# Attention and SwiGLU layer on one core: staging in two tags, final sums spread, two queues left to the scheduler

## The chip, the cores and the metric

The kernel runs on one core of a Trainium2 chip. The metric is the device time of one execution in microseconds (us), given as the median of the runs shown.

A core has five engines that work side by side, each through its own queue of instructions in order: TensorE (PE, matmuls; its weight loads are listed as PEld), VectorE (DVE), ScalarE (ACT), GpSimd (POOL) and SyncE (SP), which issues nearly all transfers here. An instruction starts when it is at the head of its queue and the semaphores that it waits for have come.

## The reference, cut to what matters

One sequence of 2048 rows with 576 columns goes through attention with 32 query heads and 16 key heads over the last 512 keys of a cache, then through a SwiGLU MLP with 4608 hidden columns. Both are gated by vectors computed from a condition c. All data are fp32.

```
mod = (silu(c) @ w_mod).reshape(1, 6, 1, -1)          # sa, ca, ga, sb, cb, gb
h = layernorm(x) * (1 + ca) + sa
q = (h @ wq) in 32 heads of 128                       # wq: 576 x 4096
k, v = k_cache[:, :, -512:], v_cache[:, :, -512:]     # 16 heads, each used twice
o = softmax(q k^T * 128**-0.5) v                      # 2048 x 4096
x = x + ga * (o @ wo)                                 # wo: 4096 x 576
h = layernorm(x) * (1 + cb) + sb
out = x + gb * ((silu(h @ w1) * (h @ w3)) @ w2)       # w1, w3: 576 x 4608, w2: 4608 x 576
```

## The kernel before

**Split numbers.** A matmul operand is kept as a rounded high part and the low rest. `split` (L82) makes them: ACT casts the high part (L84), another engine subtracts it from the source (L85). A product is then three matmuls, or seven for the 576-deep ones.

**Attention** runs in 128 slots, one for each head and block of 512 rows: first blocks 0 and 1, then blocks 2 and 3, with the two blocks of a head in successive slots. A slot has four steps t. In each, PE makes the scores of 128 rows (`scores`, L315 to L317), turns an earlier slot's exponentials (`turn`, L335), projects the next slot's q (`query`, L266) and multiplies an earlier slot's result with wo (`attend_out`, `back`, L282). ACT casts the turned exponentials to their high part (pth, L336), DVE subtracts the low part (ptl, L342), and DVE adds the result into acc (L366). Per head wq is loaded three slots and split two slots ahead of its first use (wh on ACT, wl on POOL with L85); wo is loaded (L229), weighted by gate_a (POOL, L773) and split into o. Per two heads K and V are loaded the same way. gate_a and gate_b are made on PE (`mod_rows`, L146); gate_b belongs to slot 9.

**Preparation.** The MLP needs its weights as operand sets of a seven-product scheme with sums and differences of quarter blocks, high and low parts each. These sets are made during attention and written to DRAM. For each of 36 chunks f of 128 hidden columns `load_raw` (L471, L474) loads the raw blocks, POOL makes sums (L483 to L487), and `make_set` makes seven sets, each with an ACT cast (L489) into a staging tile wmade, two POOL subtractions (L490, L491) and a write on SP (L492, to wd). For each pair of chunks `load_rows` (L519) loads rows of w2, POOL weights them by gate_b and makes sums (L538 to L543), and `keep` stages seven tiles omade: ACT cast L525, POOL L526, write L529 to od. Staging tiles are buffers of tag xn, ST = 4 of them. A cast can start only when the write of the tile four before it has landed.

The 385 items are put into the steps of slots 8 to 56, 66 to 74 (`early`, five items to four steps) and 85 to 116 (`late`). Raw loads are issued six steps ahead of the first set, row loads eleven steps ahead of the first tile. Their tag hs has seven buffers, which also hold w_mod blocks and normalized rows.

**MLP.** It runs in two pairs of row blocks, 36 groups each, one group per chunk (pair 0: groups 0 to 35, pair 1: 36 to 71). d counts the pairs of chunks, j is the chunk in it. A group has seven products (`product`, L570: sums py and px), and after each a few of the 14 units of `down` (L648: pe and pf) for the chunk pair before, whose results DVE adds into sums (L636). `act_steps` splits the activations for these units (aah, aal, akv), mostly on POOL. Weight sets come on SP by L563, w2 rows by L558.

At the end of a pair the sums are combined: `finish` has five POOL additions per 128-row tile (L592 to L596), `finish_first` one (L603), and for pair 0 the results are stored (L607). `down` calls these directly behind units 6 to 13 of d = 17 and d = 34. The last chunk pair has its own path, `plain` (L658).

**What sets the order.** ORDERED (L34) lists the engines whose instructions are issued in the order in which the program writes them. An engine that is not in the list is ordered by the scheduler, which runs the program through a model of its own and gives a free engine the earliest written operation that is ready there. Buffers of a tag are handed out in written order. `at(i, t, task)` puts a task behind step t of slot i, or behind product t of group ("m", g); t = -1 is ahead of the first.

Of the kernel before, what the change touches and what calls it, by code (L numbers as in the profile page):

```python
# [9 lines left out]
F32R = mybir.dt.float32r  # L10
# [6 lines left out]
P = 128  # L17
D = 576
DC = 4
# [4 lines left out]
ST = SB // P  # L24
# [5 lines left out]
HALF = D // 2  # L30
EPS = 1e-5
PB, QB, RB, HB = 4, 1, 3, 7

ORDERED = {mybir.EngineType.PE, mybir.EngineType.DVE, mybir.EngineType.Activation, mybir.EngineType.Pool, mybir.EngineType.SP}  # L34
SCALE = float(DH) ** -0.5


# [1 line left out]
def tile_block(  # L39
# [14 lines left out]
    nc = tc.nc  # L54
# [405 lines left out]

    wdram = {(f, k): dram.tile([P, DC + 1, P], F32, name=f"wd{f}{k}") for f in range(NF) for k in ORDER}
    works = {}

    def load_raw(f):

# [11 lines left out]
    def make_set(f, n):  # L477


        a11, a12, a21, a22, s1, s2 = (works[f][:, k] for k in range(6))  # L480
        k, x = (("p1", a11), ("p2", a12), ("p4", a22), ("p5", s1), ("p6", s2), ("p7", a21), ("p3", a12))[n]
        if n == 0:
            nc.gpsimd.tensor_add(s1, a21, a22)  # L483
            nc.gpsimd.tensor_sub(s2, s1, a11)
        elif n == 2:
            nc.gpsimd.tensor_sub(a21, a11, a21)
            nc.gpsimd.tensor_sub(a12, a12, s2)  # L487
        t = pool.tile([P, DC + 1, P], F32R, tag="xn", name="wmade", bufs=ST)
        nc.scalar.copy(t[:, :3, :], x)  # L489
        nc.gpsimd.tensor_sub(t[:, 3:, :], x[:, :2, :], t[:, :2, :].bitcast(F32))  # L490
        nc.gpsimd.tensor_sub(t[DR:, 2, :], x[DR:, 2, :], t[DR:, 2, :].bitcast(F32))  # L491
        nc.sync.dma_start(wdram[f, k][:, :, :], t.bitcast(F32))  # L492
        if n == 6:
            del works[f]
# [6 lines left out]
    G = NF // 2  # L501
# [19 lines left out]

    def keep(x, to, also=None):

        t = pool.tile([P, 2, HALF], F32R, tag="xn", name="omade", bufs=ST)
        nc.scalar.copy(t[:, 0, :], x)  # L525
        nc.gpsimd.tensor_sub(t[:, 1, :], x, t[:, 0, :].bitcast(F32))  # L526
        for dst in (to, also):
            if dst is not None:
                nc.sync.dma_start(dst, t.bitcast(F32))  # L529
# [47 lines left out]
    def split_act(d, k, x, eng):  # L577
        tags = ("ah", "al") if k in ("p7", "p4", "p6") else ("kv", "kv")
        hi, lo = [pool.tile([P, SB], F32R, tag=t, name=f"a{t}", bufs=8 if t == "kv" else 3) for t in tags]
        split(hi, lo, x, eng)  # L580
        halves[d, k] = hi, lo
# [6 lines left out]
    def finish(pair, t, eng):  # L588

        m15, m6 = msums[pair][0][t], msums[pair][1][t // 2][:, t % 2, :]  # L590
        a = half_split(acc[2 * pair + 1][:, t, :])
        eng.tensor_add(m6, m6, m15[:, 0, :])  # L592
        eng.tensor_add(a[:, 1, :], a[:, 1, :], m6)
        eng.tensor_add(a[:, 0, :], a[:, 0, :], a[:, 1, :])
        eng.tensor_add(a[:, 1, :], a[:, 1, :], m15[:, 1, :])
        eng.tensor_add(m15[:, 1, :], m15[:, 1, :], m6)  # L596
        if pair == 0:
            store_out(1, t)

    def finish_first(pair, t, eng):  # L600

        a = half_split(acc[2 * pair][:, t, :])
        eng.tensor_add(a, a, msums[pair][0][t])  # L603

    def store_out(b, t):
        lo = b * SB + t * P
        nc.sync.dma_start(out[0, lo : lo + P, :], acc[b][:, t, :])  # L607
# [3 lines left out]
    def down(d, u):  # L611

        pair = d // G
        lane[0] += 1
        ps = lane[1][lane[0] % 2]
        if u < 4:
            q, t = 0, u
            jobs = [("p4", 0, t), ("p7", 1, t)]
            into = half_split(acc[2 * pair + 1][:, t, :])
        elif u < 6:  # L620
            q, t = 1, u - 4
            jobs = [("p6", 0, 2 * t), ("p6", 0, 2 * t + 1)]
            into = msums[pair][1][t]
        elif u < 10:
            q, t = 2, u - 6
            jobs = [("p1", 0, t), ("p5", 1, t)]
            into = msums[pair][0][t]
        else:
            q, t = 3, u - 10
            jobs = [("p2", 0, t), ("p3", 1, t)]  # L630
            into = half_split(acc[2 * pair][:, t, :])
        multiply(ps, [(halves[d, k], osets[d, q][:, i], r) for k, i, r in jobs])
        if d % G == 0 and q in (1, 2):
            nc.vector.tensor_copy(into, ps[:, :, :HALF])
        else:
            nc.vector.tensor_add(into, ps[:, :, :HALF], into)  # L636
        if d == G - 1 or d == 2 * G - 2:
            if q == 2:
                finish(pair, t, nc.gpsimd)
            elif q == 3 and pair == 0:  # L640
                finish_first(0, t, nc.vector)
                store_out(0, t)

    def multiply(ps, jobs):
        for h, ((lh, ll), w, r) in enumerate(jobs):
# [18 lines left out]
    def act_steps(g, k):  # L664

        d, j = divmod(g, 2)
        x, pool_sub = acts[d], nc.gpsimd.tensor_sub
        if d == 2 * G - 1 and j == 1:
            if k in (0, 1):
                split_act(d, ("p1", "p7")[k], x[0, k], nc.vector)  # L670
            elif k in (5, 6):
                split_act(d, ("p4", "p2")[k - 5], x[1, 6 - k], nc.vector)
        elif j == 0 and d and d - 1 in acts:
            o = acts[d - 1]
            if k == 1:
                split_act(d - 1, "p6", o[0, 0], nc.gpsimd)
            elif k == 2:
                split_act(d - 1, "p5", o[0, 1], nc.gpsimd)
            elif k == 3:
                split_act(d - 1, "p2", o[1, 0], nc.gpsimd)  # L680
                pool_sub(o[1, 0], o[1, 0], o[0, 0])
            elif k == 6 or d == 2 * G - 1 and k == 4:
                split_act(d - 1, "p3", o[1, 0], nc.gpsimd)
                del acts[d - 1]
        elif j == 1:
            if k == 0:
                x["s3"] = pool.tile([P, SB], F32, tag="ql", name="s3", bufs=QB)
                pool_sub(x["s3"], x[0, 0], x[0, 1])
            elif k == 2:
                split_act(d, "p7", x.pop("s3"), nc.gpsimd)  # L690
            elif k == 4:
                split_act(d, "p1", x[0, 0], nc.gpsimd)
            elif k == 5:
                split_act(d, "p4", x[1, 1], nc.vector)
            elif k == 6:
                nc.gpsimd.tensor_add(x[0, 1], x[0, 1], x[1, 1])
                pool_sub(x[0, 0], x[0, 1], x[0, 0])


    AFTER = (1, 1, 1, 1, 2, 0, 1)  # L700
# [56 lines left out]
    def at(i, t, task, *args):  # L757

        tasks.setdefault((i, t), []).append((task, args))
# [31 lines left out]


    last_group = len(groups) - 1
    early = [4 * i + t for lo, hi in ((8, 57), (66, 75)) for i in range(lo, hi) for t in range(ST)]
    late = [4 * i + t for i in range(85, 117) for t in range(ST)]
    items = []
    for p in range(G + 1):
# [41 lines left out]
    for pair, i in ((0, 2 * HQ + 23), (1, ("m", 14))):  # L839
        at(i, 0, split_x, pair)  # L840
    at(("m", 2), -1, begin_sums, 0)
    at(("m", 2 * G + 2), -1, begin_sums, 1)

    def begin_h(b):
        hT[b] = new_h()
# [184 lines left out]
```

## Time and profile before

| | before |
|---|---|
| median of three runs | 3114.67 us |
| lowest and highest run | 3114.42 and 3119.19 us |
| the profiled execution | 3117.57 us |
| its span, first to last instruction | 3115.7 us |
| mean granted TensorE clock | 0.995 |
| PE busy | 98% |

The rows of the next section but one come from this execution. In windows each row is one stretch (from:to in us), its length, the busy us and count of each engine, the granted clock, the DMA engines' busy share and GB/s. In rows of the chain of waits the columns are start and duration in us and what ran. In rows of a timeline they are the same, with the idle time of the engine before the row, and what ended it, in brackets. In groups of instructions: engine, operation, output <- input, shapes and count, then busy us and mean ns of one, then idle time of the engine just before them with what ended most of it. In waits: engine and line, what it waited for, us in total, times, longest.

### The profile page before, as it was taken

The page shows a single profiled execution, that of the slowest core. Times are in us where ns is not written, and L with a number is a line of the kernel's source. Part 1 is how long each engine was busy: PE and PEld are TensorE (multiplying, and loading weights), DVE is VectorE, ACT ScalarE, POOL GpSimd, SP SyncE. Part 2 cuts the span into 40 slices and gives each one's busy share as a digit, 9 for nine tenths or more (in the row PEclk, how much of TensorE's full clock was granted, in tenths as well). Part 3 has the DMA queues.
Part 4 walks back from the last instruction along what each step waited for, and adds up shares of the span by engine and source line. Part 5 has one row for each costly group of instructions (what it writes and reads, how often), then busy time and mean ns, then how long its engine had stood idle before and what let it go on. Part 6 is the DMA issues. An engine that isn't in the chain of part 4 may idle for free.

```text
span 3115.7 us, 47901 instructions
## 1 busy us (share of the span) xinstructions
PE 3045.8 (98%) x16948; PEld 2662.8 (85%) x16948; DVE 2000.1 (64%) x3041; ACT 1479.4 (47%) x3107; POOL 1634.1 (52%) x1657
## 2 busy tenths in 40 slices
PE   7999999999999999999999999999999999999998
PEld 6878888888888888888888888888888888888887
DVE  6766666666777777767777766555555555555555
ACT  5556656655666655566666553333333222322321
POOL 3277877777743752476675113445555453433444
PEclk9999999999999999999999999999999999999999
DMA  4255455545521432245443235667666765666663
GB/s 141 78 170 192 156 187 167 180 167 186 172 76 56 164 119 66 96 170 172 147 161 122 63 139 169 215 227 247 237 232 221 281 223 192 200 206 194 200 204 119
DMA packets 330128, 523.13 MB, mean 168 GB/s; under 512 B 32800, under 2 KB 161824, under 8 KB 328096
## 3 DMA queue, kind: packets, MB, share of 16 engines
q1 hardware_dynamic: 329280, 520.06, 50.2%
q8 instruction: 135, 2.21, 0.3%
q14 instruction: 105, 0.86, 0.1%
q10 hardware_dynamic: 608, 0.00, 0.0%
HBM read 369.76 MB, written 150.18 MB: 167 GB/s over the span
## 4 chain that ended last, share of the span: by engine, by line
PE 77%; POOL 9%; DMA 4%; issue 3%; SPq 3%; DVE 3%; ACT 2%; POOLq 0%; ACTq 0%; DVEq 0%
PE py L570 14%; PE px L570 11%; PE pe L282 9%; PE pq L266 7%; PE pf L648 6%; PE pe L648 6%; PE pt L335 5%; PE po L353 3%; PE po L351 3%; PE po L352 3%; PE pss L317 3%; PE pss L315 3%; PE pss L316 3%; POOL wmade L490 2%; SPq L474 1%
## 5 line engine op out<-in xcount | busy, mean ns | idle before, releaser
L325 ACT ACTIVATE p<-pss,nm 128x512 f32<-128x512 f32 x512 | 352.9, 689 | 341.0 <-DVE nm L319 340.5
L570 PE MATMUL py<-hset,wset 128*128 128x512 f32 x2016 | 507.2, 391 | 2.1 <-DMA wset<-wd0p 2.1
L366 DVE SCALAR_TENSOR_TENSOR acc<-pe,r,acc 128x576 f32<-128x576 f32 x512 | 416.6, 814 | 48.0 <-PE pe L282 42.4
L319 DVE TENSOR_REDUCE nm<-pss 128x1 f32<-128x512 f32 x512 | 349.5, 683 | 111.3 <-PE pss L317 111.2
L570 PEld LDWEIGHTS py<-hset,wset 128*128 128x128 f32 x2016 | 362.9, 188 | 61.2 <-issue 2.6
L342 DVE TENSOR_TENSOR ptl<-pt,pth 128x512 fp32r<-128x512 f32 x512 | 349.5, 683 | 75.1 <-ACT pth L336 74.0
L282 PEld LDWEIGHTS pe<-o,oth 128*128 128x128 f32 x2048 | 326.2, 189 | 71.7 <-DVE acc L366 29.1
L570 PE MATMUL px<-hset,wset 128*128 128x512 f32 x1512 | 382.6, 393 | 0.0
L282 PE MATMUL pe<-o,oth 128*128 128x288 f32 x2048 | 358.4, 297 | 20.4 <-DVE acc L366 19.1
L570 PEld LDWEIGHTS px<-hset,wset 128*128 128x128 f32 x1512 | 277.3, 189 | 49.6
L336 ACT CAST pth<-pt 128x512 fp32r<-128x512 f32 x512 | 300.9, 588 | 30.5 <-PE pt L335 28.1
L335 PE MATMUL pt<-ident,p 128*128 128x128 f32 x2048 | 307.9, 273 | 4.6 <-DVE ptl L342 2.6
L85 POOL TENSOR_TENSOR akv<-u,akv 128x512 fp32r<-128x512 f32 x140 | 179.9, 1295 | 238.5 <-ACT akv L84 237.0
L335 PEld LDWEIGHTS pt<-ident,p 128*128 128x128 f32 x2048 | 249.8, 141 | 18.6 <-issue 3.0
L315 PE MATMUL pss<-kh,qh 128*128 128x512 f32 x512 | 245.2, 479 | 0.7 <-ACT qh L84 0.7
L85 DVE TENSOR_TENSOR otl<-po,oth 128x512 fp32r<-128x512 f32 x128 | 88.6, 692 | 228.6 <-ACT oth L84 228.6
L490 POOL TENSOR_TENSOR wmade<-wraw,wmade 128x256 fp32r<-128x256 f32 x252 | 186.1, 738 | 89.2 <-ACT wmade L489 44.1
L282 PE MATMUL pe<-o,otl 128*128 128x288 f32 x1024 | 219.7, 296 | 0.0
L351 PE MATMUL po<-pth,vh 128*128 128x512 f32 x512 | 203.3, 397 | 11.2 <-ACT pth L336 11.2
L84 ACT CAST oth<-po 128x512 fp32r<-128x512 f32 x128 | 74.9, 585 | 282.1 <-PE po L353 282.1
L353 PE MATMUL po<-ptl,vh 128*128 128x512 f32 x512 | 204.1, 399 | 0.8 <-DVE ptl L342 0.8
L317 PE MATMUL pss<-kh,ql 128*128 128x512 f32 x512 | 203.1, 397 | 0.0
(179 smaller groups left out, 6540.3 us busy)
## 6 DMA issues: line engine op xcount, KB each, us to landing
oset<-od SPq DMA_DIRECT2D x106, 576.0 KB, 4.8
od<-omade SPq DMA_DIRECT2D x133, 288.0 KB, 2.5
oraw<-in_A_wo SPq DMA_DIRECT2D x64, 288.0 KB, 3.1
wraw<-in_B_w SPq DMA_DIRECT2D x144, 128.0 KB, 2.5
wraw<-in_A_wq SPq DMA_DIRECT2D x64, 256.0 KB, 3.2
w2raw<-in_B_w SPq DMA_DIRECT2D x38, 288.0 KB, 3.6
oset<-od SPq DMA_DIRECT2D x35, 288.0 KB, 3.3
wraw<-in_B_w SPq DMA_DIRECT2D x288, 32.0 KB, 1.9
```

The source lines that it names most:

```text
L282: nc.tensor.matmul(E[:, h, :HALF], a[:, rows], b[:, h * HALF : (h + 1) * HALF], start=n == 0, stop=n == 2)
L315: nc.tensor.matmul(pss, st["qh"][:, rows], kh, start=True, stop=False)
L319: nc.vector.tensor_reduce(nm, pss, axis=AX.X, op=ALU.max, negate=True)
L325: nc.scalar.activation(p, pss, AF.Exp, bias=nm, accum_out=st["l"][:, t : t + 1])
L335: nc.tensor.transpose(ps[:, j, :], p[:, j * P : (j + 1) * P], ident)
L336: nc.scalar.copy(st["pt"][0][:, :, t * P : (t + 1) * P], ps)
L342: nc.vector.tensor_sub(pt[1][:, :, cols], state[i]["t"], pt[0][:, :, cols].bitcast(F32))
L351: nc.tensor.matmul(po, vh[:, j, :], pt[0][:, j, :], start=j == 0, stop=False)
L353: nc.tensor.matmul(po, vh[:, j, :], pt[1][:, j, :], start=False, stop=j == KC - 1)
L366: nc.vector.scalar_tensor_tensor(a, E[:, :, :HALF], st["r"][:, t : t + 1], a, op0=ALU.mult, op1=ALU.add)
L570: nc.tensor.matmul(ps, w[:, a, :], h[:, b, :], start=start and n == 0, stop=stop and n == 6, skip_group_check=True)
L648: nc.tensor.matmul(ps[:, h, :HALF], a[:, rows], w[:, b, :], start=m == 0, stop=m == 2)
```

## The change

- ORDERED loses POOL and SP.
- `staging` hands out the tiles wmade and omade by turns from tag w (8 buffers, shared with wh and wl) and tag xn (4).
- `early` begins with slot 10. So 280 items lie in the early stretches instead of 290, and 105 in the late one instead of 95.
- `finish` and `finish_first` are taken out of `down`. Each tile's call is put behind a product of its own in groups 37 and 38, and 70 and 71. begin_sums(1) moves from the start of group 38 to behind its product 3.
- At the last chunk pair, akv of p3 is split behind product 3 instead of 4; the low part of p2's akv goes from DVE to POOL. At d = 34 the two additions L696 and L697 go from POOL to DVE.

```diff
@@ -31,7 +31,7 @@
 EPS = 1e-5
 PB, QB, RB, HB = 4, 1, 3, 7
 
-ORDERED = {mybir.EngineType.PE, mybir.EngineType.DVE, mybir.EngineType.Activation, mybir.EngineType.Pool, mybir.EngineType.SP}
+ORDERED = {mybir.EngineType.PE, mybir.EngineType.DVE, mybir.EngineType.Activation}
 SCALE = float(DH) ** -0.5
 
 
@@ -460,6 +460,13 @@
 
     wdram = {(f, k): dram.tile([P, DC + 1, P], F32, name=f"wd{f}{k}") for f in range(NF) for k in ORDER}
     works = {}
+    staged = [0]
+
+    def staging(shape, name):
+
+        staged[0] += 1
+        tag, bufs = (("xn", ST), ("w", 8))[staged[0] % 2]
+        return pool.tile(shape, F32R, tag=tag, name=name, bufs=bufs)
 
     def load_raw(f):
 
@@ -485,7 +492,7 @@
         elif n == 2:
             nc.gpsimd.tensor_sub(a21, a11, a21)
             nc.gpsimd.tensor_sub(a12, a12, s2)
-        t = pool.tile([P, DC + 1, P], F32R, tag="xn", name="wmade", bufs=ST)
+        t = staging([P, DC + 1, P], "wmade")
         nc.scalar.copy(t[:, :3, :], x)
         nc.gpsimd.tensor_sub(t[:, 3:, :], x[:, :2, :], t[:, :2, :].bitcast(F32))
         nc.gpsimd.tensor_sub(t[DR:, 2, :], x[DR:, 2, :], t[DR:, 2, :].bitcast(F32))
@@ -521,7 +528,7 @@
 
     def keep(x, to, also=None):
 
-        t = pool.tile([P, 2, HALF], F32R, tag="xn", name="omade", bufs=ST)
+        t = staging([P, 2, HALF], "omade")
         nc.scalar.copy(t[:, 0, :], x)
         nc.gpsimd.tensor_sub(t[:, 1, :], x, t[:, 0, :].bitcast(F32))
         for dst in (to, also):
@@ -601,6 +608,10 @@
 
         a = half_split(acc[2 * pair][:, t, :])
         eng.tensor_add(a, a, msums[pair][0][t])
+
+    def finish_rows(t):
+        finish_first(0, t, nc.vector)
+        store_out(0, t)
 
     def store_out(b, t):
         lo = b * SB + t * P
@@ -634,12 +645,6 @@
             nc.vector.tensor_copy(into, ps[:, :, :HALF])
         else:
             nc.vector.tensor_add(into, ps[:, :, :HALF], into)
-        if d == G - 1 or d == 2 * G - 2:
-            if q == 2:
-                finish(pair, t, nc.gpsimd)
-            elif q == 3 and pair == 0:
-                finish_first(0, t, nc.vector)
-                store_out(0, t)
 
     def multiply(ps, jobs):
         for h, ((lh, ll), w, r) in enumerate(jobs):
@@ -669,7 +674,7 @@
             if k in (0, 1):
                 split_act(d, ("p1", "p7")[k], x[0, k], nc.vector)
             elif k in (5, 6):
-                split_act(d, ("p4", "p2")[k - 5], x[1, 6 - k], nc.vector)
+                split_act(d, ("p4", "p2")[k - 5], x[1, 6 - k], (nc.vector, nc.gpsimd)[k - 5])
         elif j == 0 and d and d - 1 in acts:
             o = acts[d - 1]
             if k == 1:
@@ -679,7 +684,7 @@
             elif k == 3:
                 split_act(d - 1, "p2", o[1, 0], nc.gpsimd)
                 pool_sub(o[1, 0], o[1, 0], o[0, 0])
-            elif k == 6 or d == 2 * G - 1 and k == 4:
+            if k == (3 if d == 2 * G - 1 else 6):
                 split_act(d - 1, "p3", o[1, 0], nc.gpsimd)
                 del acts[d - 1]
         elif j == 1:
@@ -693,8 +698,9 @@
             elif k == 5:
                 split_act(d, "p4", x[1, 1], nc.vector)
             elif k == 6:
-                nc.gpsimd.tensor_add(x[0, 1], x[0, 1], x[1, 1])
-                pool_sub(x[0, 0], x[0, 1], x[0, 0])
+                eng = nc.vector if d == 2 * G - 2 else nc.gpsimd
+                eng.tensor_add(x[0, 1], x[0, 1], x[1, 1])
+                eng.tensor_sub(x[0, 0], x[0, 1], x[0, 0])
 
 
     AFTER = (1, 1, 1, 1, 2, 0, 1)
@@ -791,7 +797,7 @@
 
 
     last_group = len(groups) - 1
-    early = [4 * i + t for lo, hi in ((8, 57), (66, 75)) for i in range(lo, hi) for t in range(ST)]
+    early = [4 * i + t for lo, hi in ((10, 57), (66, 75)) for i in range(lo, hi) for t in range(ST)]
     late = [4 * i + t for i in range(85, 117) for t in range(ST)]
     items = []
     for p in range(G + 1):
@@ -839,7 +845,12 @@
     for pair, i in ((0, 2 * HQ + 23), (1, ("m", 14))):
         at(i, 0, split_x, pair)
     at(("m", 2), -1, begin_sums, 0)
-    at(("m", 2 * G + 2), -1, begin_sums, 1)
+    at(("m", 2 * G + 2), 3, begin_sums, 1)
+
+    for t in range(ST):
+        at(("m", 2 * G + 1), 2 * t, finish, 0, t, nc.gpsimd)
+        at(("m", 2 * G + 1 + t // 2), (3, 5, 0, 2)[t], finish_rows, t)
+        at(("m", 4 * G - 2 + (t + 1) // 4), (4, 5, 6, 0)[t], finish, 1, t, nc.gpsimd)
 
     def begin_h(b):
         hT[b] = new_h()
```

The order of PE's instructions is the same before and after. Line numbers of the changed kernel are seven higher in the preparation (L499 is L492 of before, L490 is L483, L497 L490, L526 L519, L533 L526) and other numbers further down (L599 to L603 are L592 to L596).

SP around slots 8 to 10, before: the writes of sets (wmade), the load of w2 rows (w2raw) and of wo (oraw).

```order
L492 DMA wd0p1_105<-wmade_1844 128x640
L492 DMA wd0p2_106<-wmade_1849 128x640
L519 DMA w2raw_1854<-in_B_w2 128x576 x2
L229 DMA oraw_1887<-in_A_wo 128x576
L492 DMA wd0p4_111<-wmade_1891 128x640
```

The same place of the changed kernel, where kvraw is K or V and the first wraw is wq:

```order
L229 DMA oraw_1846<-in_A_wo 128x576
...
L239 DMA kvraw_1971<-in_A_k_cache 128x4x128
L215 DMA wraw_2004<-in_A_wq 128x4x128
L217 DMA wraw_2004<-in_A_wq 64x128 x2
L526 DMA w2raw_2155<-in_B_w2 128x576 x2
L239 DMA kvraw_2141<-in_A_v_cache 128x4x128
L229 DMA oraw_2187<-in_A_wo 128x576
L499 DMA wd0p1_105<-wmade_2145 128x640
L499 DMA wd0p2_106<-wmade_2150 128x640
```

The w2raw load stood ahead of the oraw load of the same slots; now an oraw load and the K and wq loads are ahead of it, and the sets are written later.

POOL in the early stretch, before: the sums on a raw chunk (L483, L484) stand where the first set of that chunk is made, behind the seven omade tiles of the pair before.

```order
L526 TENSOR_TENSOR omade_5442<-w2raw_4764,omade_5442 128x288
L773 TENSOR_TENSOR oraw_5376<-oraw_5376,gate_a_766 128x576
L483 TENSOR_TENSOR wraw_5243<-wraw_5243 128x384
L484 TENSOR_TENSOR wraw_5243<-wraw_5243 128x384
L490 TENSOR_TENSOR wmade_5512<-wraw_5243,wmade_5512 128x256
```

The same place of the changed kernel; wraw_4998 is the current chunk and wraw_5517 the next one:

```order
L497 TENSOR_TENSOR wmade_5446<-wraw_4998,wmade_5446 128x256
L498 TENSOR_TENSOR wmade_5446<-wraw_4998,wmade_5446 64x128
L490 TENSOR_TENSOR wraw_5517<-wraw_5517 128x384
L491 TENSOR_TENSOR wraw_5517<-wraw_5517 128x384
L493 TENSOR_TENSOR wraw_5517<-wraw_5517 128x384
L497 TENSOR_TENSOR wmade_5480<-wraw_4998,wmade_5480 128x256
L498 TENSOR_TENSOR wmade_5480<-wraw_4998,wmade_5480 64x128
L85 TENSOR_TENSOR o_5510<-oraw_5309,o_5510 128x576
L533 TENSOR_TENSOR omade_5513<-w2raw_5049,omade_5513 128x288
```

Three sums on the next chunk now come before the last set of the current one, and before the omade tiles.

POOL in the last groups, before: the low part of p3's akv behind two tiles of finishing sums.

```order
L681 TENSOR_TENSOR u0_32351<-u0_32351,u0_32203 128x512
L592 TENSOR_TENSOR sums156_27666<-sums156_27666,sums15_27665 128x288
L593 TENSOR_TENSOR acc3_86<-acc3_86,sums156_27666 128x288
...
L596 TENSOR_TENSOR sums15_27665<-sums15_27665,sums156_27666 128x288
L85 TENSOR_TENSOR akv_32592<-u0_32351,akv_32591 128x512
```

The same place of the changed kernel:

```order
L686 TENSOR_TENSOR u0_32351<-u0_32351,u0_32203 128x512
L85 TENSOR_TENSOR akv_32556<-u0_32351,akv_32555 128x512
L599 TENSOR_TENSOR sums156_27754<-sums156_27754,sums15_27753 128x288
L600 TENSOR_TENSOR acc3_86<-acc3_86,sums156_27754 128x288
```

The akv of p3 is now directly behind the subtraction L686 that makes its source, ahead of all finishing sums.

## Rows read from the trace of the kernel before

**Rows 1.** Page, busy time, share of the span and instructions by engine.

```profile
PE 3045.8 (98%) x16948; PEld 2662.8 (85%) x16948; DVE 2000.1 (64%) x3041; ACT 1479.4 (47%) x3107; POOL 1634.1 (52%) x1657
```

**Rows 2.** Windows, slots 9, 10–56, 66–74, 85–116: length, busy PE PEld DVE ACT POOL, clock.

```profile
166.00:191.70 25.70, 18.98 (x92) 15.95 (x91) 10.35 (x16) 9.32 (x22) 14.44 (x19) 0.87 0.43 147
191.70:875.60 683.90, 662.14 (x3712) 570.70 (x3711) 467.01 (x743) 422.18 (x969) 518.07 (x631) 1.00 0.54 178
1004.80:1134.90 130.10, 127.23 (x712) 110.00 (x711) 94.32 (x164) 82.51 (x190) 96.84 (x117) 0.99 0.49 165
1274.70:1716.40 441.70, 441.70 (x2529) 388.72 (x2528) 314.01 (x489) 271.76 (x613) 293.07 (x311) 1.00 0.46 152
```

**Rows 3.** Window of slots 10 to 56, score matmul L315 alone (PE, PEld).

```profile
191.70:875.60 683.90, 89.82 (x188) 35.85 (x188) 1.00 0.54 178
```

**Rows 4.** Groups of ACT instructions, slots 10 to 56, the two preparation casts.

```profile
L489 ACT CAST wmade<-wraw 128x384 fp32r<-128x384 f32 x158 | 78.4, 513 | 16.1 <-DMA wd4p<-wmade 3.8 <-DMA wd12p<-wmade 3.7 <-DMA wd2p<-wmade 3.3
L525 ACT CAST omade<-w2raw 128x288 fp32r<-128x288 f32 x77 | 32.8, 432 | 58.2 <-DMA od<-omade 30.9 <-POOL wmade L490 8.0 <-DMA wd17p<-wmade 4.1
```

**Rows 5.** Chain of waits, 234 to 244 us (start us, us, what).

```profile
236.55 5.67 DMA wd2p<-wmade
...
242.25 0.24 ACT pth L336
...
243.98 0.40 PE pe L282
```

**Rows 6.** Waits of SP's queue, 160 to 180 us.

```profile
SPq L519 <- PE pe L146: 9.5, 1, 9.5
```

**Rows 7.** Chain of waits, 164 to 186 us.

```profile
169.36 2.22 PE pe L146 x8
...
172.49 6.01 DMA oraw<-in_A_wo
```

**Rows 8.** Waits of SP's queue, 2490 to 2526 us, the pair switch.

```profile
SPq L607 <- POOL acc L595: 24.8, 4, 9.9
```

**Rows 9.** Timeline of PE, 2505 to 2530 us.

```profile
2506.85 1.75 PE L570 MATMUL px<-hset,wset 128*128 128x512 f32 x7
...
2513.02 0.53 PE L648 MATMUL pf<-oset,aah 128*128 128x288 f32 x2 [2.03 <-ACT aah L84]
...
2514.38 2.64 PE L570 MATMUL px<-hset,wset 128*128 128x512 f32 x7
...
2520.07 1.85 PE L570 MATMUL py<-hset,wset 128*128 128x512 f32 x7 [1.61 <-DMA wset<-wd0p]
```

**Rows 10.** Tile acc on DVE, 2490 to 2530 us: ns minimum/median/maximum.

```profile
L603 DVE TENSOR_TENSOR acc<-acc,sums x4: 760/1344/1829, 2503.1 to 2516.6; 128x576 f32<-128x576 f32 x4
```

**Rows 11.** Timeline of PE, 3045 to 3116 us, the tail.

```profile
3054.90 0.53 PE L648 MATMUL pe<-oset,aah 128*128 128x288 f32 x2 [0.98 <-DVE acc L636]
...
3076.07 0.61 PE L648 MATMUL pf<-oset,akv 128*128 128x288 f32 x1 [4.84 <-POOL akv L85]
...
3077.91 3.19 PE L570 MATMUL px<-hset,wset 128*128 128x512 f32 x7
...
3103.87 0.50 PE L648 MATMUL pf<-oset,aah 128*128 128x288 f32 x2 [2.36 <-issue]
```

**Rows 12.** Timeline of POOL, 3048 to 3080 us.

```profile
3065.88 0.81 POOL L592 TENSOR_TENSOR sums<-sums,sums 128x288 f32<-128x288 f32 x1
...
3074.75 1.26 POOL L85 TENSOR_TENSOR akv<-u,akv 128x512 fp32r<-128x512 f32 x1
```

**Rows 13.** Timeline of DVE, 3096 to 3110 us.

```profile
3102.41 0.69 DVE L85 TENSOR_TENSOR akv<-u,akv 128x512 fp32r<-128x512 f32 x1 [0.68 <-ACT akv L84]
```

**Rows 14.** Groups of POOL instructions, slots 10 to 56.

```profile
L490 POOL TENSOR_TENSOR wmade<-wraw,wmade 128x256 fp32r<-128x256 f32 x158 | 116.7, 739 | 45.0 <-issue 19.9 <-ACT wmade L489 19.7 <-POOL wmade L491 0.7
...
L483 POOL TENSOR_TENSOR wraw<-wraw 128x384 f32<-128x384 f32 x22 | 22.3, 1014 | 0.5
```

**Rows 15.** Waits, slots 10 to 56, PE on POOL's low half of wq.

```profile
PE pq L266 <- POOL wl L85: 0.6, 1, 0.6
```

## The prediction

> **What bounds the kernel now.** I read the page's table of engines first [rows 1]. TensorE (PE) is busy for 98% of the span and every other engine for at most 64%, so the end moves only where PE stands idle, or where its matmuls take longer than they need.
>
> To find such places I compared stretches with the same work [rows 2]. Slots 85 to 116 (32 slots) take 441.70 us with 441.70 us of PE: 13.80 us a slot, 79 matmuls each, no idle time. Slots 10 to 56 run the same 79 matmuls a slot (3712 in 47 slots; the 188 first score matmuls, four a slot, give the count [rows 3]), and take 683.90 us. At 13.80 that would be 648.7, so 35.2 us are lost: 21.8 as idle PE (683.90 − 662.14) and 13.4 as the same matmuls taking longer. Slots 66 to 74 lose 130.10 − 124.2 = 5.9 in the same way. Slot 9 takes 25.70 us; the eight matmuls of gate_b add 2.22 to its 13.80 [rows 7], so it loses 25.70 − 16.02 = 9.7.
>
> What the two long stretches share, and the calm one lacks, is dense preparation of the MLP's weights. ScalarE's (ACT's) two casts of it, L489 and L525, wait 16.1 + 58.2 = 74.3 us in slots 10 to 56, nearly all of it for the DMA that empties the staging buffer which they are to fill [rows 4]. The chain of waits shows how this reaches PE [rows 5]: a write takes 5.67 us, the L489 cast waits for its buffer, the cast of the attention weights (pth, L336) is queued behind it on ACT, VectorE (DVE) waits for that, and PE for DVE. ACT works in written order, so a full staging pool stops PE. Of the 74.3 us, 35.2 reach the end.
>
> Slot 9 has another cause. SP's queue stands 9.5 us at the load of w2raw, whose buffer is free only when gate_b's matmuls have read it [rows 6]; the load of oraw behind it goes out afterwards and takes 6.01 us [rows 7].
>
> In the MLP, PE is idle in few places: 2.03 and 1.61 us at the pair switch, with one product at 2.64 where others take 1.75 [rows 9]; and 0.98, 4.84 and 2.36 in the tail, with one product at 3.19 behind the 4.84 [rows 11].
>
> **The change, part by part.**
>
> *Staging in two tags.* Preparation casts take buffers of tag xn (4) and tag w (8) by turns. The wq halves take two w buffers a head and at most four are alive, so about four are left: staging goes from four buffers to about eight. A buffer's life may then double before ACT stops, and a write of 5.67 us fits. I expect the waits on DMA to go, and those on POOL to stay: 8.0 of 74.3 = 11% by the one such releaser that is large [rows 4]. Gain: (35.2 + 5.9) × 0.89 = 36.6. Bounds: 41.1, if all goes; nothing, if the w buffers are not free when wanted (rival C). What is late next is POOL. It is busy for 518.07 of 683.90 us, 76%; the same work in 648.7 us is 80% [rows 2]. PE waited for POOL's wl once in these 47 slots (24 heads), 0.6 us [rows 15]. In the 28 heads of the two stretches I put seven such waits, 4.2 us of loss, between none and rival A.
>
> *Two slots later, and SP in the scheduler's order.* The first row load now comes later than gate_b, and oraw is in front of it in SP's order. The 9.5 us wait and its tail go: gain 9.7; at least 9.7 − 6.0 if another wait for oraw takes its place. The ten items that move into the late stretch meet a PE without idle time and a POOL at 66% (293.07 of 441.70) [rows 2]: nothing. The five loads that move up SP's queue at the start (two of x, three of w_mod) are bounded by nothing and one landing, 6.0 us [rows 7]; I take nothing, since the K, V and wq loads that they pass are issued two and three slots ahead of their use.
>
> *Sums of the first pair spread.* In the kernel before, SP waits 24.8 us in all at the result stores for POOL's finishing sums, up to 9.9 at once [rows 8], and the weight sets behind them come late (the 1.61); the 2.03 is a DVE/ACT chain in which finishing sums occupy both POOL and DVE. With one sum per product, and the weight loads ahead of the stores, I take 4 of 2.03 + 1.61 + (2.64 − 1.75) = 4.5; bounds 0 and 4.5.
>
> *Tail.* The 4.84 us is PE waiting for akv on POOL [rows 11], which starts at 3074.75 behind ten finishing sums that began at 3065.88 [rows 12]. Now it stands in front of them: it can end at 3065.88 + 1.26 = 3067.1, while PE wants it at 3076.07 − 4.84 = 3071.2. So the idle time and the slow product behind it go: 4.84 + (3.19 − 1.75) = 6.3. At the 2.36 stall PE waits for the DVE addition queued behind an L85 on DVE, which stood 0.68 for its cast and took 0.69 [rows 13]; on POOL instead, it frees 1.4 (bounds 0 and 2.36). The two additions that move from POOL to DVE stand in front of the L636 for which PE already waits 0.98: 2 × 0.69 = 1.4 more (bounds 0, if the wait has slack elsewhere, and 1.4 plus the rule below). Tail: 6.3 + 1.4 − 1.4 = 6.3, at most 6.3 + 2.4 = 8.7.
>
> The same rows bear on a rule for those two additions. The L603 additions at the pair switch are one shape, alone 760 ns and at most 1829 ns where POOL works beside them [rows 10], so company cost up to 1.07 us. The Trainium skill, "SBUF — State Buffer", section "🎯 Summary: rules for kernel authors", says of VectorE and GpSimd together that a VectorE operation with two SBUF inputs and a GpSimd operation that reads SBUF exclude each other: the second to issue waits until the first is done. By that rule each of the two additions could also wait for one POOL operation (1.26), and the tail would gain 6.3 − 2.5 = 3.8; the trace agrees in kind (1.07 of a possible 1.26), but in the tail POOL's sums now lie later, so I keep 6.3.
>
> **Sum.** 36.6 + 9.7 + 4 + 6.3 = 56.6; less 4.2 of new waits, 52.4. The profiled execution took 3117.57 us with a span of 3115.7, and would become 3065.2. It lies 2.9 above the median of the three runs; I carry the gain over to the median: 3114.67 − 52.4 = 3062.3, say 3062.
>
> **Rivals.**
>
> *A: POOL becomes the bound.* With four more buffers ACT may run four items ahead, and POOL has four more items in front of a wl: 4 × 0.74 = 3.0 us by their larger subtraction alone [rows 14]. For it: POOL at 80%. Against it: wl is cut a slot and more before its use, and was late once in 24. If a head loses 1 us on the mean, 28 heads take 28 of the 56.6: 3114.67 − 28.6 = 3086.
>
> *B, the slower side: POOL and SP in the scheduler's order.* The scheduler orders by its own idea of durations. In its order POOL takes up three additions on the next raw chunk (each 1.01 us [rows 14]) ahead of the current chunk's last item, and SP mixes loads with writes. An engine that stands at an operation whose load has not landed holds everything behind it; a load takes some 6.0 us [rows 7]. If POOL's wl or oraw is held like that at each head, and PE with it, the loss is up to 28 × 6.0 = 168. It decides from 56.6 / 28 = 2.0 us a head. At half of the heads: 84 lost, 3114.67 − 56.6 + 84 = 3142. Against it: the raw chunk is loaded six steps (1.5 slots, 20.7 us) ahead of its use, three times 6.0.
>
> *C: the staging does not do what it says.* If the w buffers are held by wq halves that PE still reads, a cast waits there as it did in xn. Then only slot 9 and the MLP's places gain: 9.7 + 4 + 6.3 = 20.0, 3095.
>
> *D: nothing that can be measured,* losses as large as gains: 3115.
>
> **How the numbers follow.** Forecast 0.62 (3048 to 3075), A 0.13, C 0.08, D 0.05, B 0.12. Faster takes in the forecast, A and C: 0.83; same D: 0.05; slower B: 0.12. A measurement of this kernel tells about 0.2%, 6 us, from no change. The low end: every loss named goes and nothing new comes, 41.1 + 9.7 + 4.5 + 8.7 = 64.0, 3051, and 5 us below that for matmuls that took longer at small stalls not listed: 3046. The high end takes in A and C: 3100. Left out are B, D and little else, under 2 in 10.
>
> **What would show it.** Slots 10 to 56 at 650 to 655 us instead of 684, waits before the two casts below 15 us instead of 74; slot 9 at 16 us; no gap above 1 us around the pair switch; akv on POOL ahead of the finishing sums and no 4.84. Wrong if PE waits for POOL's wl, o or oraw in many heads (A, B), or if the casts wait on PE's reading of w buffers (C).

## The result and the profile after

The changed kernel takes 3128.05 us (median of five runs, 3125.39 to 3130.94) against 3114.42 for the kernel before in the same comparison: 1.0041 times as long, 95% interval 1.0026 to 1.0055. It is slower by about 13 us where 52 us less were forecast, and it lies outside the range of 3046 to 3100. The profiled execution took 3128.05 us with a span of 3126.2 and a mean granted clock of 0.989 (before 0.995).

The engines' totals hardly differ from [rows 1]; what changed is where and how long PE waits:

```profile
PE 3044.8 (97%) x16948; PEld 2666.8 (85%) x16948; DVE 2000.5 (64%) x3042; ACT 1483.0 (47%) x3107; POOL 1633.0 (52%) x1656
```

The same stretches as in [rows 2], by slots: 9, 10 to 56, 66 to 74, 85 to 116 (length; PE, PEld, DVE, ACT, POOL; clock, DMA share, GB/s):

```profile
163.67:180.90 17.23, 16.32 (x92) 13.96 (x91) 10.44 (x16) 7.32 (x17) 8.16 (x8) 1.00 0.11 36
180.90:888.29 707.39, 667.17 (x3713) 581.56 (x3712) 467.76 (x743) 425.08 (x969) 509.05 (x622) 0.97 0.51 167
1017.85:1144.07 126.22, 124.92 (x713) 108.84 (x711) 94.14 (x164) 82.66 (x189) 90.81 (x109) 1.00 0.50 166
1289.68:1740.12 450.44, 445.66 (x2532) 390.78 (x2530) 314.13 (x488) 275.58 (x624) 299.56 (x326) 0.99 0.48 159
```

Slot 9 fell from 25.70 to 17.23 us and slots 66 to 74 by 3.9. But slots 10 to 56 rose from 683.90 to 707.39, and the late stretch from 441.70 to 450.44.

The staging did what it was to do. The two preparation casts of [rows 4] wait 10.4 us instead of 74.3, and no longer for a write (groups of ACT instructions, slots 10 to 56):

```profile
L496 ACT CAST wmade<-wraw 128x384 fp32r<-128x384 f32 x158 | 78.1, 511 | 10.4 <-POOL wraw L494 10.4
...
L532 ACT CAST omade<-w2raw 128x288 fp32r<-128x288 f32 x77 | 31.9, 431 | 0.0
```

The loss is new. In the same slots POOL now stands: the operation at the head of its queue reads a load that has not landed. PE waits 39.2 us for POOL's wl, where [rows 15] had 0.6. In the kernel before POOL waited for loads mainly at oraw, for 10.0 us (waits: us in total, times, longest; first the kernel before, then the changed one):

```profile
POOL oraw L773 <- DMA oraw<-in_A_wo: 10.0, 4, 5.4
```

```profile
POOL wraw L490 <- DMA wraw<-in_B_w: 58.5, 14, 5.8
POOL oraw L779 <- DMA oraw<-in_A_wo: 58.3, 12, 9.2
...
PE pq L266 <- POOL wl L85: 39.2, 11, 6.6
...
POOL w2raw L545 <- DMA w2raw<-in_B_w: 23.4, 6, 5.7
```

One case, in three timelines of the changed kernel around 360 us. First POOL:

```profile
348.67 1.57 POOL L533 TENSOR_TENSOR omade<-w2raw,omade 128x288 fp32r<-128x288 f32 x2
359.48 1.43 POOL L779 TENSOR_TENSOR oraw<-oraw,gate_a 128x576 f32<-128x576 f32 x1 [9.24 <-DMA oraw<-in_A_wo]
360.87 1.57 POOL L533 TENSOR_TENSOR omade<-w2raw,omade 128x288 fp32r<-128x288 f32 x2
362.39 1.01 POOL L490 TENSOR_TENSOR wraw<-wraw 128x384 f32<-128x384 f32 x1
363.49 1.00 POOL L491 TENSOR_TENSOR wraw<-wraw 128x384 f32<-128x384 f32 x1
364.44 1.00 POOL L493 TENSOR_TENSOR wraw<-wraw 128x384 f32<-128x384 f32 x1
365.40 1.53 POOL L85 TENSOR_TENSOR wl<-wraw,wh 128x640 fp32r<-128x640 f32 x1
```

SP's queue, which issues that load only now, behind a V load and six other issues:

```profile
350.93 1.75 SPq L239 DMA_DIRECT2D kvraw<-in_A_v_cache  x1
...
355.81 0.39 SPq L229 DMA_DIRECT2D oraw<-in_A_wo  x1
```

And PE, which gets wl at 366.98:

```profile
366.98 0.80 PE L266 MATMUL pq<-hT,wl 128*128 128x512 f32 x1 [3.85 <-POOL wl L85]
```

POOL is free for the next thing at 350.24 (348.67 + 1.57). It comes to the weighting of wo (L779) and stands there from before the load is issued (355.81) until it has landed; L779 starts at 359.48. Behind it wait omade tiles, three sums on the next raw chunk and, last, wl, which PE needs first. (The Trainium skill, "PSUM — Partial Sum Buffer", section "Engine vs sequencer instructions", calls the queues of ScalarE, VectorE and GpSimd strict FIFO; this row agrees: nothing of POOL ran in the 9.24 us.)

In the MLP the gains came in size as forecast. At the pair switch PE idles 0.51 and 0.86 us where [rows 9] had 2.03 and 1.61 (timeline of PE):

```profile
2532.43 0.54 PE L653 MATMUL pf<-oset,aah 128*128 128x288 f32 x2 [0.51 <-ACT aah L84]
...
2536.43 0.53 PE L653 MATMUL pe<-oset,aah 128*128 128x288 f32 x2 [0.86 <-DVE acc L647]
```

In the tail the 4.84 of [rows 11] is gone. The 0.98 has become 1.47, and in place of the 2.36 there are 0.98 and a new 1.31 (timeline of PE):

```profile
3071.84 0.53 PE L653 MATMUL pe<-oset,aah 128*128 128x288 f32 x2 [1.47 <-DVE acc L647]
...
3110.89 0.53 PE L653 MATMUL pe<-oset,aah 128*128 128x288 f32 x2 [1.31 <-DVE acc L663]
...
3112.93 0.56 PE L653 MATMUL pf<-oset,aah 128*128 128x288 f32 x2 [0.98 <-ACT akv L84]
```

### The profile page after: what moved, and what is told of

Its sections match the earlier page's. It is cut to its first block, busy times and chain, and to the rows that moved or that the text cites. A ratio compares the mean times of both kernels' runs of the same rounds, so it can differ in the third digit from the quotient of the medians.

```text
span 3126.2 us, 47869 instructions
## 1 busy us (share of the span) xinstructions
PE 3044.8 (97%) x16948; PEld 2666.8 (85%) x16948; DVE 2000.5 (64%) x3042; ACT 1483.0 (47%) x3107; POOL 1633.0 (52%) x1656
## 4 chain that ended last, share of the span: by engine, by line
PE 71%; POOL 5%; DMA 1%; issue 1%; DVE 1%; SPq 1%; ACT 1%; POOLq 0%; ACTq 0%; DVEq 0%
PE py L577 14%; PE px L577 11%; PE pe L282 8%; PE pq L266 6%; PE pf L653 6%; PE pe L653 6%; PE pt L335 4%; PE po L353 2%; PE po L352 2%; PE po L351 2%; PE pss L317 2%; PE pss L315 2%; PE pss L316 2%; PE pq L274 1%; POOL wmade L497 1%
## 5 line engine op out<-in xcount | busy, mean ns | idle before, releaser
L282 PEld LDWEIGHTS pe<-o,oth 128*128 128x128 f32 x2048 | 330.9, 190 | 49.6 <-DVE acc L366 7.1
L282 PE MATMUL pe<-o,oth 128*128 128x288 f32 x2048 | 359.5, 298 | 3.2 <-DVE acc L366 3.1
L342 DVE TENSOR_TENSOR ptl<-pt,pth 128x512 fp32r<-128x512 f32 x512 | 348.9, 682 | 16.3 <-ACT pth L336 15.8
L85 POOL TENSOR_TENSOR akv<-u,akv 128x512 fp32r<-128x512 f32 x141 | 181.5, 1297 | 241.6 <-ACT akv L84 239.0
L266 PE MATMUL pq<-hT,wl 128*128 128x512 f32 x508 | 204.1, 402 | 46.0 <-POOL wl L85 45.9
L315 PE MATMUL pss<-kh,qh 128*128 128x512 f32 x512 | 246.9, 482 | 0.7 <-ACT qh L84 0.7
L85 DVE TENSOR_TENSOR otl<-po,oth 128x512 fp32r<-128x512 f32 x128 | 88.6, 692 | 228.7 <-ACT oth L84 228.7
L282 PE MATMUL pe<-o,otl 128*128 128x288 f32 x1024 | 221.0, 297 | 0.0
L316 PE MATMUL pss<-kl,qh 128*128 128x512 f32 x512 | 203.7, 398 | 0.0
L497 POOL TENSOR_TENSOR wmade<-wraw,wmade 128x256 fp32r<-128x256 f32 x252 | 186.4, 740 | 32.0 <-ACT wmade L496 20.3
```

The source lines that it names most:

```text
L85: eng.tensor_sub(lo, src, hi.bitcast(F32))
L266: nc.tensor.matmul(ps, (wh if k < 2 else wl)[:, m, :], hT[DC + m if k == 1 else m], start=s == 0, stop=False,)
L282: nc.tensor.matmul(E[:, h, :HALF], a[:, rows], b[:, h * HALF : (h + 1) * HALF], start=n == 0, stop=n == 2)
L315: nc.tensor.matmul(pss, st["qh"][:, rows], kh, start=True, stop=False)
L342: nc.vector.tensor_sub(pt[1][:, :, cols], state[i]["t"], pt[0][:, :, cols].bitcast(F32))
```

## The experiments

**1. The order that the scheduler gives POOL and SP.** Four kernels: the changed one with both back in written order, with POOL alone, with SP alone; and the kernel before with both left free.

```diff
 # e1_ordered, from the changed kernel
-ORDERED = {mybir.EngineType.PE, mybir.EngineType.DVE, mybir.EngineType.Activation}
+ORDERED = {mybir.EngineType.PE, mybir.EngineType.DVE, mybir.EngineType.Activation, mybir.EngineType.Pool, mybir.EngineType.SP}
 # e2_pool_ordered: with Pool, without SP
 # e3_sp_ordered: with SP, without Pool
 # e4_before_free: the kernel before, without both
```

> The changed kernel with POOL and SP back in written order, all else kept. Theory 1 (the order that the scheduler gives POOL and SP holds the low half of wq, wl, behind operations whose loads have not landed): the waits of PE for wl fall from 45.9 us to under 3, slots 10 to 56 take 650 to 660 us, and the time is 3062 (3050 to 3075). Theory 2 (the doubled staging itself fills POOL's queue, or takes buffers from wl, whatever the order): PE still waits over 20 us for wl and the time stays above 3100.

> The changed kernel with POOL in written order and SP left to the scheduler. If POOL's order alone holds wl (an operation on a load that has not landed is taken early and stands at the head): 3060 to 3070, wl waits under 5 us. If SP's order makes the loads late whatever POOL does: POOL still waits over 40 us for loads, wl waits stay above 20 us and the time above 3095.

> The changed kernel with SP in written order and POOL left to the scheduler. If POOL's order alone holds wl: above 3100 with wl waits over 30 us. If SP's late loads are the cause: 3060 to 3075.

> The kernel before with only POOL and SP left to the scheduler. Theory 1: the waits for wl come in here too (over 20 us), beside part of the old staging stalls, and the time is 3130 to 3190. Theory 2: without the doubled staging no wait for wl comes in, and the time stays within 10 us of 3115.

Measured, each against the kernel before at 3116.92 us:

| kernel | us | ratio, 95% interval |
|---|---|---|
| e1: POOL and SP written | 3063.98 | 0.9831, 0.9816 to 0.9846 |
| e2: POOL written, SP free | 3062.48 | 0.9829, 0.9812 to 0.9846 |
| e3: POOL free, SP written | 3068.96 | 0.9846, 0.9831 to 0.9861 |
| e4: before, both free | 3129.07 | 1.0043, 1.0028 to 1.0058 |

Theory 1 holds and theory 2 falls: with the same staging and the same buffers but written order (e1), the kernel gains 52.9 us, and PE has no wait for wl left in slots 10 to 56. e2 comes out as e1. Below are slots 10 to 56 of e2 (windows; columns as above), and then the largest sum of POOL's waits for a transfer there. It names a write to od; no wait of POOL for oraw, a raw chunk or w2 rows is left:

```profile
182.03:833.60 651.57, 650.51 (x3713) 569.78 (x3712) 467.67 (x743) 423.52 (x969) 519.23 (x630) 1.00 0.54 181
```

```profile
POOL omade L533 <- DMA od<-omade: 7.4, 2, 5.0
```

The expectations of e2 and e3 were framed as if one engine's order alone were the cause, and that was the miss. The time of e2 lies in the range named for POOL's order alone as the cause (3060 to 3070), and that of e3 in the range named for SP's late loads alone (3060 to 3075). Since undoing either freedom brings the time back, neither is the cause by itself. In e3 the free POOL does stand at loads (slots 10 to 56 of e3), yet PE loses only 3.1 us to wl:

```profile
POOL wraw L490 <- DMA wraw<-in_B_w: 47.8, 15, 6.3
POOL oraw L779 <- DMA oraw<-in_A_wo: 14.3, 10, 3.5
...
PE pq L266 <- POOL wl L85: 3.1, 3, 2.6
```

So either freedom by itself costs little (e2 −1.5 and e3 +5.0 against e1, where the intervals overlap), and both together cost 64 us (3128.05 against 3063.98; 66.6 if each is taken against the kernel before of its own comparison). Of the 67.5 us between the profiled spans of e2 and the changed kernel (3058.7 and 3126.2), 55.8 lie in slots 10 to 56, 3.3 in slots 75 to 84 and 8.1 in the late stretch.

e4 shows the same stands in the kernel before; of its waits, in slots 10 to 56:

```profile
POOL wraw L483 <- DMA wraw<-in_B_w: 56.4, 16, 5.5
POOL oraw L773 <- DMA oraw<-in_A_wo: 44.6, 10, 6.7
...
PE pq L266 <- POOL wl L85: 11.7, 8, 3.4
```

And its window of these slots:

```profile
182.56:888.43 705.87, 668.80 (x3714) 571.12 (x3712) 463.77 (x743) 422.57 (x969) 514.97 (x630) 0.99 0.51 169
```

e4 met its expectation in part. Its time was 1 us short of the 3130 to 3190 of theory 1 and beyond the 3125 of theory 2, but PE's wait for wl is 11.7 us where over 20 were expected. It is a third of the 37.1 us that PE idles there (705.87 − 668.80); 13.1 more are waits for DVE's acc, and ACT's preparation casts still wait for writes as in [rows 4]. So with both engines free four and eight staging buffers come to the same length of slots 10 to 56 (707.39 above), but not by the same waits, and that the order alone bounds e4 is not shown.

Why both are needed is seen from the medians over the 24 heads of slots 10 to 56, worked out from the starts of L779, L85 and SP's loads in each trace, in us relative to the first score matmul of the head's first slot (L779 is L773 in the kernel before and e4; the last column counts the heads in which it runs ahead of the head's wl):

| kernel | load of oraw issued | L779 starts | wl ends | wl ready before PE's first use | L779 ahead of wl |
|---|---|---|---|---|---|
| before | −19.9 | −13.4 | −19.8 | 6.4 | 0 of 24 |
| e1 | −20.0 | −13.1 | −19.9 | 7.3 | 0 of 24 |
| e2 | −30.2 | −14.1 | −20.0 | 7.4 | 0 of 24 |
| e3 | −19.8 | −12.7 | −17.9 | 5.2 | 1 of 24 |
| the changed kernel | −27.7 | −23.2 | −14.1 | 0.2 | 24 of 24 |
| e4 | −31.3 | −24.7 | −14.8 | 1.1 | 24 of 24 |

A free SP issues the oraw load some 8 to 10 us earlier than a written one. With POOL free as well, L779 is taken 9 us earlier than in e2, and so ahead of wl instead of behind it. With only one of the two free, L779 stays behind wl. With both, wl ends 5.9 us later than in e2, and its lead, the time from its end to PE's first use, is used up at the median head (0.2 instead of 7.4). From there on a longer stand of POOL is a wait of PE.

**2. The parts alone, in the kernel before.**

```diff
 # e5_before_staging, with the function staging of the change
-        t = pool.tile([P, DC + 1, P], F32R, tag="xn", name="wmade", bufs=ST)
+        t = staging([P, DC + 1, P], "wmade")
...
-        t = pool.tile([P, 2, HALF], F32R, tag="xn", name="omade", bufs=ST)
+        t = staging([P, 2, HALF], "omade")
 # e6_before_early10
-    early = [4 * i + t for lo, hi in ((8, 57), (66, 75)) for i in range(lo, hi) for t in range(ST)]
+    early = [4 * i + t for lo, hi in ((10, 57), (66, 75)) for i in range(lo, hi) for t in range(ST)]
```

> The kernel before with only the staging by turns in xn and w; POOL and SP in written order. By the sum of the prediction this part is worth 36.6 us, by the profile of the run with everything but the free order some 35 (slots 10 to 56 fall by 30.2, slots 66 to 74 by 4.8): 3078 to 3084. Rival: staging takes w buffers or POOL time from wl, and the gain stays under 15 us.

> The kernel before with only the preparation begun at slot 10. By the prediction 9.7 us less (slot 9 at 16.0 us); by the profile of the changed kernel slots 8 and 9 together give 7.7: 3105 to 3110. Rival: with four staging buffers the ten items come back as stalls elsewhere, and the time stays within 4 us of before.

e5 took 3076.44 us against 3116.29 (0.9879, 0.9864 to 0.9894): 39.9 us less, a little more than forecast, and no sign of the rival. e6 took 3100.49 (0.9951, 0.9936 to 0.9966): 15.8 less, below the expected 3105 to 3110. Slots 8 and 9 gave 7.7 of it in the profile, as expected; slots 10 to 56 lost 23.1 us beyond 13.80 a slot instead of 35.2, though the staging there is the old one. Why the items that begin later stall less stays open. The two parts overlap: 39.9 + 15.8 and the MLP's 10.5 (below) would make 66.2, and e1, which has all, gained 52.9. Slots 8 and 9 are one place where they do: together they take 39.6 us before, 31.9 in e6 and 32.4 in e5. In e5 SP still stands 9.5 us at the row load and POOL 9.2 at oraw, but ACT's wait of 10.3 us for a write and PE's of 5.8 for acc are gone. So there, too, the stands reached PE by way of the full staging.

**3. How a standing POOL reaches PE.**

```diff
 # e7_wl_on_vector, from the changed kernel
-        split(wh, wl, raw, nc.gpsimd)
+        split(wh, wl, raw, nc.vector)
 # e8_wl_and_sums: that, and in make_set
-            nc.gpsimd.tensor_add(s1, a21, a22)
-            nc.gpsimd.tensor_sub(s2, s1, a11)
+            nc.vector.tensor_add(s1, a21, a22)
+            nc.vector.tensor_sub(s2, s1, a11)
...
-            nc.gpsimd.tensor_sub(a21, a11, a21)
-            nc.gpsimd.tensor_sub(a12, a12, s2)
+            nc.vector.tensor_sub(a21, a11, a21)
+            nc.vector.tensor_sub(a12, a12, s2)
```

> The changed kernel, POOL and SP still free, with the low half of wq (wl) subtracted by DVE instead of POOL. If POOL standing at loads reaches PE by wl alone: no wait of PE for wl above 5 us in all, slots 10 to 56 at 655 to 675 us, time 3070 to 3090 (POOL still stands at loads as long). If it reaches PE by other work of POOL too (o, vl, staging that fills): PE waits there instead, and the time stays above 3105.

> The changed kernel, POOL and SP free, with wl and the four sums on a raw chunk (L490 to L494) on DVE. In the run with wl alone on DVE, ACT waited 29.3 us for the sum L494 on POOL, and attention's casts behind it. If wl and this sum are the two ways by which a standing POOL reaches PE: 3060 to 3078, PE waits in slots 10 to 56 under 8 us in all, though POOL still stands at oraw and w2raw for 50 us or more. If a third way is left (o, staging that fills): above 3085.

e7 took 3092.89 us (0.9929, 0.9912 to 0.9946), between the two expectations: PE's waits for wl are gone, and over half of the loss with them (35 of 64 us). What is left comes by a second way (waits of e7, slots 10 to 56):

```profile
POOL wraw L490 <- DMA wraw<-in_B_w: 59.0, 14, 6.5
POOL oraw L779 <- DMA oraw<-in_A_wo: 57.0, 11, 9.0
...
ACT wmade L496 <- POOL wraw L494: 29.3, 6, 7.0
...
PE pe L282 <- DVE acc L366: 17.0, 6, 5.6
```

POOL stands as long as in the changed kernel; now an ACT cast waits for POOL's sum L494, and ACT's attention casts behind it hold DVE and PE, as the full staging did in [rows 5]. In time the two go together: each of the five waits of PE above 1 us ends 1 to 3 us behind the end of one of ACT's stands at L496.

e8 was a miss: 3152.75 us (1.0126, 1.0108 to 1.0145), slower than any other, and by its number in the range named for a third way (above 3085). But the sums on DVE, which works in written order, wait for POOL in their turn (waits of e8, slots 10 to 56):

```profile
PE pe L282 <- DVE acc L366: 33.4, 22, 7.3
DVE wraw L494 <- POOL wmade L498: 25.2, 9, 7.9
```

The experiment put a new wait on DVE, whose results PE needs in every slot, so it doesn't tell whether a third way exists.

**4. Taking one stand away.**

```diff
 # e9_gate_on_vector, from the changed kernel
-        nc.gpsimd.tensor_mul(into[key], into[key], gates[kind])
+        nc.vector.tensor_mul(into[key], into[key], gates[kind])
 # e10_gate_early, from e2 (POOL written, SP free)
-        at(*(i - 1, 0) if i > 2 else (1, 1), gate, wos, key, "a")
+        at(*(i - 2, 1) if i > 2 else (1, 1), gate, wos, key, "a")
```

> The changed kernel, POOL and SP free, with the weighting of wo by gate_a (L779) on DVE, so that POOL never stands at the load of oraw (63 us of its 153 in slots 8 to 56) but still at the raw chunks and w2 rows. If PE's loss grows with the time that POOL stands: between the two, 3080 to 3110, PE's waits for wl 10 to 25 us. If the loads of the preparation alone hold wl as long: above 3115. If DVE, in written order, stands at oraw instead: DVE waits for it over 10 us, and the gain is lost there.

> The run with POOL in written order and SP free (3062), with one thing moved: the weighting of wo by gate_a (L779) stands directly behind the issue of its load, three steps earlier, so that POOL stands at each oraw for its landing, as it does when it is free, while the rest of POOL's order stays written. If time that POOL stands is lost to PE one way or another: 60 us or more of waits for oraw in slots 10 to 56, PE waits for wl above 15 us, time 3085 to 3120. If short stands spread over the heads are absorbed by wl's lead, and only long or clustered ones reach PE: the waits for oraw come, PE's waits for wl stay under 5 us, and the time is 3060 to 3072.

e9 took 3076.27 us against 3115.2 (0.9874, 0.9859 to 0.9889), 4 us below what was expected for a partial gain: with L779 off POOL, 52 of the 64 us are back although both engines are free. PE's waits for wl fall to a quarter, just below the 10 to 25 us named (waits of e9, slots 10 to 56):

```profile
POOL wraw L490 <- DMA wraw<-in_B_w: 38.3, 12, 5.9
POOL w2raw L545 <- DMA w2raw<-in_B_w: 23.5, 8, 5.3
...
PE pq L266 <- POOL wl L85: 9.1, 3, 3.7
```

POOL's other stands are as long as they were: the idle time ahead of L490 is 63.2 us in all (the row names 38.3, and the rest is put down to other transfers, though nearly all of it, too, ends within 0.3 us of the raw chunk's landing), against 59.1 in the changed kernel. DVE did not stand at oraw; there L779 runs 10.9 us ahead of the head's first score matmul (median), after wl in all 24 heads, and wl's lead is 3.9 us. The move also takes the 1.43 us of each L779 off POOL. That POOL simply had too much to do is spoken against by e2, where it has all of it and PE has no wait for wl.

e10 does not settle what it was for. It took 3066.19 us (0.9833, 0.9817 to 0.9849), but the stands that it was to make, 60 us or more, did not come: POOL in written order reaches L779 a median of 10.1 us after its load was issued, and waits for oraw 3.4 us in all:

```profile
POOL oraw L779 <- DMA oraw<-in_A_wo: 3.4, 2, 2.1
```

So how much spread standing wl's lead would absorb stays open. It shows that this earlier place does no harm while wl stays ahead of L779 on POOL, as it does in all 24 heads.

## Why the prediction was wrong, point by point

- **Staging (36.6).** Right: 39.9 alone (e5), and the waits of the casts fell to 10.4 us, under the 15 named. Slots 10 to 56 take 651.57 us in e2, within the 650 to 655 named.
- **Two slots later (9.7).** Slots 8 and 9 together gave 7.7 us; slot 9 went to 17.23, not 16.0. In the changed kernel SP still stands 9.5 us at the row load, but oraw is no longer behind it. The cause was half seen: by e5 (above) the doubled staging alone frees most of the same time. Alone in the kernel before the part was worth 15.8, the rest of it in slots where staging gains as well. The ten items that moved were put at nothing, and cost 0.4 us: the late stretch takes 442.2 us in e1 and e2. The 450.44 of the changed kernel belongs to the free order.
- **Pair switch (4).** From the first product of group 38 to that of group 39: 23.61 us before, 19.11 after, a gain of 4.5.
- **Tail (6.3).** From the first product of group 70 to the last instruction: 64.35 us before, 58.36 after, a gain of 6.0. The 4.84 went as forecast. The two terms of 1.4 were both too large and nearly cancelled, in part by luck: the two additions on DVE cost 1.47 − 0.98 = 0.5, and the waits of 0.33 and 2.36 around p2's akv became 1.31 and 0.98, a gain of 0.4. The two additions took 0.68 and 0.69 us with POOL idle, so the rule on VectorE and GpSimd had nothing to bite on there. A multiplication of the same shape (L747 at 3107.11), begun 0.3 us behind a POOL addition (L610), took 1.68 and is part of the new 1.31. In e2 the same multiplication began 0.18 us ahead of such an addition; it took 0.78, the POOL addition 1.90 instead of 1.44, and PE's wait there was 0.88. That is as the Trainium skill, "SBUF — State Buffer", section "🎯 Summary: rules for kernel authors", would have it: of two such operations the one that issues second waits for the first. In the same way the 760 ns of [rows 10] were not taken alone: a POOL addition began 0.06 us behind them and took 1.37 instead of 0.81.
- **POOL and SP in the scheduler's order: the step that failed.** The sum held "seven such waits, 4.2 us" for all waits for wl. Measured are 64 us for the free order: e1, with everything else, gained 52.9 where 52.4 was forecast, and the changed kernel lost 13. So the sum fitted the kernel with written order (where the 4.2 did not come either, and single terms were off by up to 2 us both ways), and the free order cancelled it. The 4.2 was set between none and rival A, and what stood against A was that "wl is cut a slot and more before its use". The trace of before shows a lead of 6.4 us (median of 24 heads), under half a slot. The two slots ahead at which wq is split count to the head's first slot, but PE uses wl a slot earlier, where it projects q for it.
- **Rival B** named the mechanism, at a chance of 0.12 and a price of 3142 for 3128. From e2 to the changed kernel slots 10 to 56 alone lost 707.39 − 651.57 = 55.8 us, 2.3 a head over 24 heads; 2.0 was named as the point of decision. Its reason was half right. POOL does stand at raw chunks, but by e9 the dear stand is that at oraw, taken ahead of wl; with the raw chunks alone (e9) 12 of the 64 us are left. The argument against it (a raw chunk is loaded 20.7 us ahead of its use) counted steps of the written program. In the trace of before, the last load of a chunk is issued a median of 11.4 us ahead of the first sum on it; in the changed kernel POOL is free for that sum 0.6 us before the load is issued. Nor did I compare the place of L779 with that of wl in the new POOL order, where it could have been read.
- **Rival A** (POOL full) is refuted: e2 has POOL busy for 519.23 of 651.57 us, 80% as forecast, and no wait for wl worth a microsecond.
- **Rival C** is refuted by e5 and e2: in slots 10 to 56 no preparation cast waits there for a buffer that PE reads or a write empties.

## What to carry to other kernels

Background work that is given more buffers no longer stops the engine that fills them; see then in which order the next engine takes it, and whether the one operand that the bound engine needs soon is behind work that waits for a load. An engine left to a scheduler is ordered by loads that have landed in the scheduler's model, not on the chip. Free the queue that issues the loads and the queue that consumes them together only after comparing the place of each urgent operation in the new order with its lead in the trace of before, from the end of the operation that makes it to its first use. When a change mixes parts, a trial with one part undone (here one line) shows at once that the others were worth 53 us.

## What was not expected of the hardware's behaviour

Freed separately, the two queues cost −1.5 and +5.0 us; together 64. And where PE was made to wait in single gaps of up to 6.6 us, the matmuls behind them took longer too. In the case above the granted clock was 1.00 from 355 to 363 us, and after the 3.85 us in which PE stood it was 0.50 from 367 to 370 (1.2 of 2.4 GHz): four matmuls of L282 took 0.69 us at 357.85 and 1.16 at 367.57. Over slots 10 to 56 the granted clock was 0.97 instead of 1.00, and of the 58.8 us beyond 13.80 a slot 40.2 were idle time and 18.6 the same matmuls taking longer.
